# Attention with decay and a softplus FFN on one core: k of each head loaded by two half transfers, and new scheduler tables

## Chip, core, metric

One core of a Trainium2 chip (trn2). The metric is the device time of one execution in microseconds (us); lower is better. The engines are TensorE (PE, with its weight loads shown as PEld), VectorE (DVE), ScalarE (ACT), GpSimd (POOL) and SyncE (SP), which issues nearly all DMAs here. Each engine runs its instructions in order and waits on semaphores.

## What is computed

```python
# q, k, v: (8, 8, 576, 64) float32; f: (8, 8, 576); w_in: (512, 2048), w_out: (2048, 512), float64
scores = q @ k.T / sqrt(64)
cum = cumsum(log(clip(f, 1e-4, 1)))
scores = where(causal, scores + cum[i] - cum[j], -1e9)
attn = exp(scores - max); attn = attn / (sum(attn) + 1e-9)
x = (attn @ v), heads side by side: (4608, 512)
h = x @ w_in
out = softplus(h) @ w_out
```

The batch has 8 sequences of 8 heads, 576 tokens of 64 dimensions each. The host passes q and k transposed, as one array `qkT[b, d, head, q or k, token]`, so that a head's k is 64 rows of 576 floats (2304 bytes).

## The kernel before

**Precision.** Most products are done in a reduced float kind (fp32r), and a float is split into a high part (a rounding copy, "hi") and the rest ("lo", a subtraction). For q and k, both lie twice in a tile of 128 partitions, once in rows 0 to 63 and once in 64 to 127, so that a tile `T` of four planes can be filled with high and low parts in different rows.

**Stages.** The first sequence is done in plain float32 pieces while weights are loaded and split (0 to about 85 us). Then come 56 whole heads (sequences 1 to 7), each a job of `attention`; between their matmuls stand those of the FFN for blocks of 512 tokens that are already finished (85 to 975 us). The last 2048 tokens go through two "super blocks", whose matrix products are arranged as seven products in place of eight (975 us to the end).

**A whole head.** `load` issues the DMAs of q (two transfers of 64 partitions, line 886, in small reversed pieces) and of k (line 891), each into a buffer of the tag `raw`, of which there are two. `prepare` makes `T` from them: casts `T<-k` and `T<-q` through the helper of line 329, on ACT or DVE (128 rows of k, 128 rows of q, and 64 rows of k a second time), and two subtractions on POOL (line 931). When these are done the `raw` buffers are free, and the next head's q and k can be issued. Two rows with the cumulated decay come from `aug_d` into T by DMA (lines 920 and 923). Of `T` there are two buffers.

Then, for each tile of query rows: scores on PE (lines 976, 977, `s<-T`), the mask and the row's minimum of the negated score on DVE (line 981, `s<-s,cmask`, and 1018, `negm`), the weights on ACT (line 1025, `p` for the two short tiles and `pb` for the long ones), sums and scaling (lines 1038, 1039, 1053, 1055, on any of three engines), the transpose on PE (line 1118, `b<-ident,pb`), its high part (`ph`, ACT, or DVE line 1137 for a small block) and low part (`pl`, DVE, line 1140), and the product with v on PE (line 1265, `o`). v is loaded as `vr` (lines 826 and 831) and split into `vhl` (line 903). The FFN's first product is line 1506 (`h`), its gate on ACT is `e` (line 325), split into `gh` and `gl` (line 1550), partly stored to DRAM (`g_d`, line 1554), and the second product is line 1580 (`acc`).

**What sets the order.** Operations are given to a `Plan`, each with the engines that may run it, an estimated cost on each, and what it needs. `run` places one operation after another: of those that are ready in a window of 700, the one whose planned start, less a number for its kind, is smallest. This number is looked up in the table `SOONER`; the table `RATHER` adds to the cost of a kind on one engine and so moves work between engines. The kind is the name of the function that emits it. Planned costs decide only the order; on the chip, semaphores decide when each runs. SP's DMAs are in the planned order as well. The planner counts a DMA of 288 KB as landed 2.1 us after its slot on SP.

```python
    key = s and (s[0] - op.sooner, op.rank)
    return each * (n - 1) + 2.1 + kb / n / RATE - on_dma(kb, n, eng).cost
```

Of the kernel before, what the change touches and what calls it, by code (L numbers as in the profile page):

```python
# [48 lines left out]
S_FROM, S_EACH = 9, 4  # L49

SOONER = {
    "<lambda>": 0.26,
    "attention.finish.shift": 0.15,
    "attention.finish_stats.scale": -0.17,
    "attention.load.k": 0.22,
    "attention.load_quad.<lambda>": 6,
    "attention.load_v.v": 0.21,
    "attention.output_tiled.put": 0.09,
    "attention.prepare.decay_rows": -0.14,
    "attention.split_v.v_hi": -0.68,  # L60
    "attention.split_v.v_lo": -0.04,
    "attention.stat_tile.row_min": 0.04,
    "attention.stat_tile.shift": 0.11,
    "attention.weights.keep": 0.19,
    "attention.weights.spread": -1.63,
    "decay.load": 5.45,
    "decay.split": 2.5,
    "ffn_block.gate.hi_part": -0.27,
    "ffn_block.gate.keep": 3.7,
    "ffn_block.gate.lo_part": -0.52,  # L70
    "ffn_block.gate.raw": -0.12,
    "ffn_block.second.load": 3.23,
    "ffn_block.split_stored.load": 0.22,
    "ffn_block.split_x.lo_part": 0.45,
    "ffn_block.up_part.load": 0.31,
    "load_f64.clip": -0.06,
    "load_f64.join": 0.17,
    "load_f64.low": -0.42,
    "load_f64.scale": 0.22,
    "load_f64.sign": -0.04,  # L80
    "split_w_in.hi_part": 0.13,
    "split_w_in.keep": -0.23,
    "split_w_in.lo_part": -0.23,
    "split_w_out.lo_part": -0.29,
    "store_x.store": 4.21,
    "super_blocks.down_out.keep": -1.38,
    "super_blocks.down_set.split.high": -0.17,
    "super_blocks.gate.raw": 0.07,
    "super_blocks.gate.store": 0.47,
    "super_blocks.lay_out.hold.begin": 0.29,  # L90
    "super_blocks.lay_w.load": 1.48,
    "super_blocks.lay_w.split.lo": 0.55,
    "super_blocks.lay_w.step.go": 0.02,
    "super_blocks.lay_x.less.go": 0.57,
    "super_blocks.lay_x.load": 5.93,
    "super_blocks.lay_x.split.high": 0.36,
    "super_blocks.lay_x.split.low": 0.74,
    "super_blocks.super_block.ups.sum_of.go": 0.07,
    "turn_mask.turn": 6,
}  # L100
RATHER = {
    ("attention.finish_stats.scale", "ACT"): 0.85,
    ("attention.finish_stats.scale", "DVE"): 0.08,
    ("attention.finish_stats.scale", "POOL"): -0.39,
    ("attention.prepare.<lambda>", "ACT"): 0.15,
    ("attention.split_v.v_hi", "ACT"): 0.94,
    ("attention.weights.hi_part", "DVE"): 1.02,
    ("attention.weights.keep", "ACT"): -0.4,
    ("attention.weights.keep", "DVE"): -0.48,
    ("ffn_block.gate.hi_part", "ACT"): 1.61,  # L110
    ("ffn_block.gate.hi_part", "DVE"): 1.87,
    ("load_f64.sign", "POOL"): 1.23,
    ("put_out.<lambda>", "ACT"): 0.87,
    ("set_rows.<lambda>", "DVE"): 1.51,
    ("split_w_in.hi_part", "DVE"): 0.6,
    ("split_w_out.hi_part", "ACT"): 0.42,
    ("split_w_out.hi_part", "DVE"): 0.53,
    ("super_blocks.down_set.split.high", "ACT"): 1.12,
    ("super_blocks.lay_sums.<lambda>", "DVE"): -0.49,
    ("super_blocks.lay_sums.<lambda>", "POOL"): -0.17,  # L120
    ("super_blocks.lay_w.split.hi", "ACT"): -0.75,
    ("super_blocks.lay_w.split.hi", "DVE"): -0.75,
    ("super_blocks.lay_w.split.lo", "POOL"): 1.66,
    ("turn_mask.turn", "DVE"): -0.42,
}


def kind_of(emit):

    return emit.__qualname__.split("<locals>.", 1)[-1].replace("<locals>.", "")  # L130
# [15 lines left out]
class Plan:  # L146
# [14 lines left out]
    def add(self, on, emit, after=(), takes=(), lag=None, loose=False):  # L161
        op = Op(on, emit, after, takes, lag)
        op.loose = loose
        kind = kind_of(emit)
        op.sooner = SOONER.get(kind, 0.0)
        if len(op.on) > 1:
            op.on = [x._replace(bias=x.bias + RATHER.get((kind, x.eng), 0.0)) for x in op.on]
        op.at = len(self.ops)
        op.rank = op.at + self.late
        self.ops.append(op)  # L170
        for t in set(takes):
            self.queue[t].append(op)
        for d in op.after:
            d.users.append(op)
        return op
# [107 lines left out]
def on_dma(kb, n=1, eng="SP"):  # L283

    return On(eng, max(0.6 * n, kb / RATE) if eng == "SP" else 1.5 * n)


def dma_lag(kb, n=1, eng="SP"):
    each = 0.6 if eng == "SP" else 1.5
    return each * (n - 1) + 2.1 + kb / n / RATE - on_dma(kb, n, eng).cost  # L290
# [26 lines left out]
def last_first(x, n=64):  # L317

    *lead, (_, w) = x.ap
    return bass.AP(x.tensor, x.offset + w - n, [*lead, [-n, w // n], [1, n]])  # L320
# [12 lines left out]
def tile_decay_attention_softplus_ffn(  # L333
# [39 lines left out]
                x32=2, ps=2, wl=2, vhl=3, vraw=1, raw=2, one=2)  # L373
    plan = Plan(BUFS | dict(T0=4, stat=4, p=2, xh0=1, xh1=1, xl0=1))
    add, give = plan.add, plan.give

    def joined():
        parts = []

        def row(e):  # L380
            for part in parts:
                part(e)

        op = add(On("PE", 0.0), row)
        op.parts = parts
        return op
# [11 lines left out]
    def add_dma(emit, kb, n=1, eng="SP", **more):  # L398
        return add(on_dma(kb, n, eng), emit, lag=dma_lag(kb, n, eng), **more)
# [9 lines left out]
    def buf(tag, shape, name, dtype=F32):  # L409
        return pool.tile(shape, dtype, tag=tag, name=name, bufs=BUFS[tag])  # L410
# [91 lines left out]
    def exchange(e):  # L502
# [12 lines left out]
            lambda e, x=x, v=v: e.mul(x, ident[0:BH, 0:BH], v) if e is nc.scalar  # L515
# [261 lines left out]
    def attention(job):  # L777

        b, heads = job["b"], job["heads"]
# [29 lines left out]
        st = {}  # L809
# [71 lines left out]
        def load():  # L881
            def q(e):
                st["q"] = buf("raw", [P, S], f"q{n}")
                for r in (0, 64):
                    out = st["q"][r : r + 64].rearrange("p (n t) -> p n t", t=64)
                    e.dma_start(out=out, in_=last_first(qkT[b, :, heads[0], 0]))

            def k(e):
                st["k"] = buf("raw", [P, S], f"k{n}")
                x = qkT[b, :, heads[0], 1]  # L890
                e.dma_start(out=st["k"], in_=bass.AP(x.tensor, x.offset, [[0, 2], *x.ap]))

            st["ql"] = add_dma(q, 288, 2, takes=("raw",))
            st["kl"] = add_dma(k, 288, takes=("raw",))

        def split_v():
            def v_hi(e):
# [427 lines left out]
        def loads():  # L1325
            if quad:
                load_quad()
            elif pair:
                st["T"] = T_of[heads[0]]
                st["vr"], st["V"], st["vtag"] = V_of[heads[0]]  # L1330
            else:
                (load32 if plain else load)()
                load_v()
# [1432 lines left out]
```

## Time and profile before

| | us |
|---|---|
| three runs | 1317.85, 1315.25, 1317.53 (median 1317.53) |
| profiled execution | 1319.71 |
| its span, first to last instruction | 1317.8 |
| mean granted clock of PE | 0.949 |
| PE busy in the span | 1170.3 (89%) |

In a profile's rows, L891 is line 891 of the kernel. In lists of groups, `out<-in` names the tiles, x is the count, and three numbers a/b/c are the shortest, median and longest duration in ns. "Idle before" is time in which the engine stood, and what ended it. In lists of waits the three numbers are us in total, times, and the longest. The chain is the work that ended last, followed back from the end, each step to what released it.

### The profile page before, as it was taken

To read this page: it belongs to the slowest core of one execution; us is meant where nothing else is said; L and a number is where in the kernel's file an instruction comes from. 1 tells how busy PE (TensorE), PEld (TensorE's weight loads), DVE (VectorE), ACT (ScalarE), POOL (GpSimd) and SP (SyncE) were. 2 spreads that over 40 slices of the span, in tenths; PEclk is the share of its full clock that TensorE was granted. 3 is DMA by queue.
4 is the path that set the end of the run, shared out by engine and by line. 5 is a ranking of instruction groups with operands and counts; after the bars stand their busy time and mean duration, and the time that the engine had idled before them with its cause. 6 is when DMAs were issued, how large, how long until landed. Compare 5 with 4: busy or idle time off the path is not lost.

```text
span 1317.8 us, 21604 instructions
## 1 busy us (share of the span) xinstructions
PE 1170.3 (89%) x6764; PEld 989.3 (75%) x6764; DVE 915.1 (69%) x2534; ACT 785.7 (60%) x1906; POOL 449.3 (34%) x445
## 2 busy tenths in 40 slices
PE   9998878898887789887888878888899999999998
PEld 7766677776666677776677667776787878799998
DVE  7877677775565667574565665665767599899784
ACT  7866566666555577665566655665665475554432
POOL 4224455444333335443334332433412014411110
PEclk9999888898889899899898998988999999999999
DMA  8786454344446444444444463544357677644441
GB/s 222 239 228 187 139 161 147 95 146 125 117 117 177 122 142 148 143 127 138 130 139 124 122 178 105 148 138 124 119 188 205 201 234 232 182 136 136 125 136 66
DMA packets 219186, 200.53 MB, mean 152 GB/s; under 512 B 84704, under 2 KB 187392, under 8 KB 219072
## 3 DMA queue, kind: packets, MB, share of 16 engines
q1 hardware_dynamic: 219048, 199.15, 51.2%
q8 instruction: 53, 0.87, 0.3%
q14 instruction: 61, 0.50, 0.1%
q10 hardware_dynamic: 24, 0.02, 0.0%
HBM read 141.17 MB, written 57.84 MB: 151 GB/s over the span
## 4 chain that ended last, share of the span: by engine, by line
PE 38%; DMA 34%; DVE 14%; ACT 5%; POOL 3%; issue 3%; SPq 3%; DVEq 0%; POOLq 0%; ACTq 0%
DMA k<-in_qkT 25%; PE late_E L2387 6%; PE late_E L2050 5%; PE h L1506 4%; PE acc L1580 4%; PE o L1265 3%; DMA vr<-in_vR 3%; PE b L1118 2%; DVE pl L1140 2%; ACT T L329 2%; POOL T L931 2%; PE late_D L2050 1%; PE late_D L2387 1%; PE late_C L2387 1%; PE late_B L2387 1%
## 5 line engine op out<-in xcount | busy, mean ns | idle before, releaser
L981 DVE CUSTOM_DVE_ANT_0 s<-s,cmask 128x288 f32<-128x288 f32 (+6 forms) x320 | 136.8, 443 | 73.1 <-PE s L977 43.9
L931 POOL TENSOR_TENSOR T<-k,T 64x576 fp32r<-64x576 f32 x56 | 80.0, 1429 | 297.4 <-DVE negm L1018 137.0
L1025 ACT ACTIVATE pb<-s,negm 128x288 f32<-128x288 f32 (+5 forms) x272 | 143.4, 530 | 46.0 <-DVE negm L1018 42.0
L976 PE MATMUL s<-T 128*128 128x192 f32 (+1 forms) x336 | 108.2, 328 | 25.7 <-ACT p L1025 8.4
L1140 DVE TENSOR_TENSOR pl<-b,ph 128x512 fp32r<-128x512 f32 x168 | 108.2, 662 | 25.9 <-ACT ph L329 24.8
L329 ACT CAST ph<-b 64x128 fp32r<-64x128 f32 x224 | 103.0, 489 | 38.5 <-PE b L1118 37.3
L1118 PE MATMUL b<-ident,pb 128*128 128x128 f32 (+2 forms) x280 | 50.6, 259 | 68.0 <-DVE ph L1137 52.9
L977 PE MATMUL s<-T 68*128 68x192 f32 (+1 forms) x336 | 103.8, 312 | 4.0 <-DMA T<-aug_d 4.0
L1265 PE MATMUL o<-ph,vhl 128*128 128x512 f32 x336 | 95.4, 321 | 10.2 <-ACT ph L329 4.8
L1025 ACT ACTIVATE p<-s,negm 128x192 f32<-128x192 f32 (+1 forms) x112 | 40.7, 363 | 104.9 <-DVE negm L1018 104.0
L903 POOL TENSOR_TENSOR vhl<-vr,vhl 128x384 fp32r<-128x384 f32 x56 | 58.3, 1041 | 122.2 <-ACT vhl L329 69.8
L1506 PE MATMUL h<-xh,wl 128*128 128x512 f32 (+1 forms) x320 | 99.7, 400 | 0.0
L976 PEld LDWEIGHTS s<-T 128*128 128x128 f32 (+1 forms) x336 | 65.3, 194 | 44.6 <-ACT p L1025 14.6
L1118 PEld LDWEIGHTS b<-ident,pb 128*128 128x128 f32 (+2 forms) x280 | 34.2, 141 | 83.6 <-DVE ph L1137 61.2
L931 POOL TENSOR_TENSOR T<-q,T 64x576 fp32r<-64x576 f32 x56 | 80.7, 1441 | 34.7 <-DVE negm L1018 10.7
L1265 PE MATMUL o<-pl,vhl 128*128 128x512 f32 x224 | 75.6, 381 | 14.0 <-DVE pl L1140 13.6
L1265 PEld LDWEIGHTS o<-ph,vhl 128*128 128x128 f32 x336 | 71.1, 212 | 20.1 <-ACT ph L329 5.1
L1506 PE MATMUL h<-xl,wih 128*128 128x512 f32 (+1 forms) x320 | 86.2, 394 | 0.0
L1118 PE MATMUL b<-halves,pb 128*128 128x128 f32 x512 | 86.0, 286 | 0.0
L1506 PE MATMUL h<-xh,wih 128*128 128x512 f32 (+1 forms) x320 | 85.6, 391 | 0.0
L329 DVE CAST T<-k 128x576 fp32r<-128x576 f32 (+1 forms) x35 | 16.1, 464 | 98.8 <-DMA k<-in_qkT 97.7
L329 ACT CAST T<-k 64x576 fp32r<-64x576 f32 (+1 forms) x77 | 51.4, 673 | 55.4 <-DMA k<-in_qkT 52.0
(749 smaller groups left out, 3583.5 us busy)
## 6 DMA issues: line engine op xcount, KB each, us to landing
wl<-wil_d SPq DMA_DIRECT2D x40, 512.0 KB
raw_d<-e SPq DMA_DIRECT2D x64, 256.0 KB
q<-in_qkT SPq DMA_DIRECT2D x112, 144.0 KB
k<-in_qkT SPq DMA_DIRECT2D x56, 288.0 KB
vr<-in_vR SPq DMA_DIRECT2D x64, 160.0 KB
x_d<-x SPq DMA_DIRECT2D x28, 288.0 KB
g_d<-gh SPq DMA_DIRECT2D x56, 128.0 KB
g_d<-gl SPq DMA_DIRECT2D x56, 128.0 KB
```

The costliest lines, as they stand in the source:

```text
L329: (e.tensor_copy if hasattr(e, "tensor_copy") else e.copy)(out, in_)
L931: e.tensor_sub(t[rows, i, :], st[x][rows], tb[rows, j, :])
L976: e.matmul(o, qA[:, S - end : S - q0], kA[:, a:z], start=True, stop=False)
L977: e.matmul(o, qB[0:ST, S - end : S - q0], kB[0:ST, a:z], start=False, stop=True)
L981: e.tensor_tensor_reduce(out=box["o"], in0=box["o"], in1=cmask[0:n_q, right - w : right], scale=-0.125, scalar=m0 if i else 3.0e38, op0=AL ...
L1025: e.activation(o, box["o"], AF.Softplus, bias=m1, scale=-1.0, accum_out=acc)
L1118: e.transpose(box["ps"][0 : x.shape[1], at : at + one.shape[1]], x, one)
L1140: e.tensor_sub(box["l"], box["ps"][:, 0:w], box["h"].bitcast(F32))
L1265: e.matmul(boxes[gi]["ps"][0:m, a:z], st["vhl"][:, c, 0:m], pbox[which][:, o : o + z - a], start=gi in fresh and which == "h", stop=gi == ...
L1506: e.matmul(o, l, r, start=m == 0, stop=m == 11)
L2050: e.matmul(banks[to], stationary(x, j), at(b, y, j), start=start and m == 0, stop=m == 5, skip_group_check=not start,)
L2387: e.matmul(like(o, y), x, y, start=q == 0 and f_ == 0 and m == 0, stop=q == NQ - 1 and f_ == 1 and m == 2,)
```

## The change

The load of k is written as two transfers. Before, the source was given an outer dimension of 2 with step 0, so that one transfer filled all 128 partitions. Now each half of the partitions has a transfer of its own from the same 64 rows, and the planner counts two issues.

```diff
             def k(e):
                 st["k"] = buf("raw", [P, S], f"k{n}")
-                x = qkT[b, :, heads[0], 1]
-                e.dma_start(out=st["k"], in_=bass.AP(x.tensor, x.offset, [[0, 2], *x.ap]))
+                for r in (0, 64):
+                    e.dma_start(out=st["k"][r : r + 64], in_=qkT[b, :, heads[0], 1])
 
             st["ql"] = add_dma(q, 288, 2, takes=("raw",))
-            st["kl"] = add_dma(k, 288, takes=("raw",))
+            st["kl"] = add_dma(k, 288, 2, takes=("raw",))
```

Both tables have other numbers, nearly all of them; two lines of each:

```diff
-    "attention.load.k": 0.22,
+    "attention.load.k": 1.91,
...
-    "attention.split_v.v_hi": -0.68,
+    "attention.split_v.v_hi": -0.65,
...
+    ("ffn_block.gate.lo_part", "DVE"): 1.72,
...
+    ("split_w_in.hi_part", "ACT"): -1.85,
```

The name of a kind gets a suffix that the plan doesn't set, so kinds stay as they were:

```diff
-        kind = kind_of(emit)
+        kind = kind_of(emit) + getattr(self, "phase", "")
```

Three places of the new order follow (SP, the casts on DVE and ACT, and POOL), all at the same head, whose q and k are numbered 51 (it is issued at 661.55 us and 662.91 us in the profile before). The number behind the last underscore is a running number and differs between the kernels.

On SP, where this head's q and k are issued. Before:

```order
L886 DMA q51_7075<-in_qkT 64x9x64 x2
L891 DMA k51_7095<-in_qkT 128x1x576
L1371 DMA out_0<-ob4_2_7078 128x512
L1554 DMA g_d_98<-gh5_2_7098 128x256
L1554 DMA g_d_98<-gl5_2_7110 128x256
```

Now:

```order
L886 DMA q51_7069<-in_qkT 64x9x64 x2
L891 DMA k51_7072<-in_qkT 64x576 x2
L1348 DMA x_d_99<-x32_5_6899 128x576
L1554 DMA g_d_98<-gh5_2_7093 128x256
L1554 DMA g_d_98<-gl5_2_7095 128x256
```

k stays right behind q; it is two issues, and the store of an earlier sequence's x comes after it, which stood ahead of q before.

The casts, first on DVE, between the row minimum of head 49's first tile (`negm`) and the low parts of head 48's weights (`pl`). Before:

```order
L981 ISA s49_0_0_7125,negm1_76<-s49_0_0_7125,cmask_74 64x64
L981 ISA negm1_76 64x1
L329 CAST T1_1386<-k51_7095 128x576
L1018 TENSOR_SCALAR negm1_76<-negm1_76 64x1
L1137 TENSOR_TENSOR ph48_0_7145<-b48_0_7128,ph48_0_7145 64x128
L1140 TENSOR_TENSOR pl48_1_7163<-b48_1_7131,ph48_1_7154 128x512
```

Now:

```order
L1137 TENSOR_TENSOR ph48_0_7149<-b48_0_7134,ph48_0_7149 64x128
L981 ISA s49_0_0_7131,negm1_76<-s49_0_0_7131,cmask_74 64x64
L981 ISA negm1_76 64x1
L1140 TENSOR_TENSOR pl48_1_7167<-b48_1_7137,ph48_1_7155 128x512
L1140 TENSOR_TENSOR pl48_2_7169<-b48_2_7144,ph48_2_7164 128x448
L1018 TENSOR_SCALAR negm1_76<-negm1_76 64x1
```

The cast of k is no longer on DVE. In the whole program DVE had 35 casts `T<-k` and 12 `T<-q`; now ACT has all 112 and 56 (77 and 44 before). DVE's 47 subtractions `gl` are now on POOL, which had 25 and has 72, while POOL's scalings of line 1055 go from 113 to 55 (`p` from 80 to 28).

And on ACT, around the casts of the same head. Before:

```order
L329 CAST ph48_2_7161<-b48_2_7139 128x448
L1025 ACTIVATE p1_92,lsum1_80<-s49_0_0_7125,negm1_76 64x64
L329 CAST T1_1386<-q51_7075 128x576
L329 CAST T1_1386<-k51_7095 64x576
L329 CAST ph48_3_7186<-b48_3_7169 128x512
```

Now:

```order
L329 CAST ph48_3_7184<-b48_3_7171 128x512
L1025 ACTIVATE p1_92,lsum1_80<-s49_0_0_7131,negm1_76 64x64
L329 CAST T1_1412<-k51_7072 128x576
L329 CAST T1_1412<-q51_7069 128x576
L329 CAST T1_1412<-k51_7072 64x576
L1025 ACTIVATE pb1_94,part1_84<-s49_4_0_7181,negm1_76 128x288
```

Three casts stand in a row where two stood, ahead of the weights of a long tile (`pb`), and the first of them waits for k.

On POOL, ahead of the subtraction of k into T. Before and now:

```order
L903 TENSOR_TENSOR vhl50_7050<-vr50_6916,vhl50_7050 128x6x64
L931 TENSOR_TENSOR T1_1386<-k51_7095,T1_1386 64x576
L931 TENSOR_TENSOR T1_1386<-q51_7075,T1_1386 64x576
L1055 TENSOR_SCALAR p1_92<-p1_92,rsum1_88 64x64
L1550 TENSOR_TENSOR gl5_4_7241<-e5_4_7123,gh5_4_7212 128x512
```

```order
L1550 TENSOR_TENSOR gl5_2_7095<-e5_2_6993,gh5_2_7093 128x512
L903 TENSOR_TENSOR vhl50_7128<-vr50_6978,vhl50_7128 128x6x64
L1550 TENSOR_TENSOR gl5_3_7153<-e5_3_7123,gh5_3_7151 128x512
L931 TENSOR_TENSOR T1_1412<-k51_7072,T1_1412 64x576
L931 TENSOR_TENSOR T1_1412<-q51_7069,T1_1412 64x576
```

Two `gl` of the FFN, each of which needs a gate `e`, now stand ahead of it.

More of the change, by code (lines that the diff above doesn't have):

```diff
@@ L51 @@
 SOONER = {
-    "<lambda>": 0.26,
-    "attention.finish.shift": 0.15,
-    "attention.finish_stats.scale": -0.17,
-    "attention.load.k": 0.22,
[L56 to L59, printed above, removed]
-    "attention.split_v.v_hi": -0.68,
-    "attention.split_v.v_lo": -0.04,
-    "attention.stat_tile.row_min": 0.04,
-    "attention.stat_tile.shift": 0.11,
-    "attention.weights.keep": 0.19,
@@ L65 @@
[L65 to L99, printed above, removed]
+    "attention.finish.shift": 0.19,
+    "attention.finish_stats.scale": -0.22,
+    "attention.load.k": 1.91,
+    "attention.load.q": 0.09,
+    "attention.load_quad.<lambda>": 0.08,
+    "attention.split_v.v_hi": -0.65,
+    "attention.stat_tile.row_min": -0.09,
@@ new lines @@
+    "attention.stat_tile.shift": 0.11,
+    "attention.weights.hi_part": 0.06,
+    "attention.weights.keep": 0.02,
+    "attention.weights.lo_part": 0.14,
+    "attention.weights.spread": -1.39,
+    "decay.load": 0.56,
+    "decay.split": 6,
+    "decay.store": -0.28,
+    "exchange": -0.2,
+    "ffn_block.gate.hi_part": -0.23,
+    "ffn_block.gate.lo_part": 3.3,
+    "ffn_block.second.load": 6,
+    "ffn_block.split_stored.hi_part": -0.16,
+    "ffn_block.split_stored.lo_part": 0.73,
+    "ffn_block.split_x.hi_part": -0.31,
@@ new lines @@
+    "ffn_block.split_x.lo_part": 4.7,
+    "load_f64.join": 0.02,
+    "load_f64.low": -0.83,
+    "load_f64.scale": -0.06,
+    "load_f64.sign": 2.43,
+    "mark": 3.39,
+    "put_out.<lambda>": -0.13,
+    "set_rows.begin": -4,
+    "split_w_in.hi_part": -0.41,
+    "split_w_in.keep": -0.31,
+    "split_w_in.lo_part": -0.2,
+    "split_w_out.hi_part": -0.26,
+    "split_w_out.lo_part": -0.06,
+    "store_x.store": 0.35,
+    "super_blocks.down_out.keep": -0.62,
+    "super_blocks.down_set.<lambda>": 0.64,
@@ new lines @@
+    "super_blocks.down_set.split.high": -0.8,
+    "super_blocks.down_set.split.low": 0.02,
+    "super_blocks.gate.store": 0.18,
+    "super_blocks.lay_sums.high": -0.22,
+    "super_blocks.lay_sums.low": 0.07,
+    "super_blocks.lay_w.split.lo": 0.74,
+    "super_blocks.lay_w.step.go": 0.44,
+    "super_blocks.lay_x.less.go": 0.34,
+    "super_blocks.lay_x.load": 4.63,
+    "super_blocks.lay_x.split.low": 6,
+    "super_blocks.super_block.product.mm": -0.61,
+    "super_blocks.super_block.ups.sum_of.go": 1.97,
@@ L100 @@
 }
 RATHER = {
[L102 to L122, printed above, removed]
@@ L123 @@
-    ("super_blocks.lay_w.split.lo", "POOL"): 1.66,
-    ("turn_mask.turn", "DVE"): -0.42,
+    ("attention.finish_stats.scale", "DVE"): -0.22,
+    ("attention.finish_stats.scale", "POOL"): -0.62,
+    ("attention.prepare.<lambda>", "ACT"): -1.44,
+    ("attention.weights.hi_part", "DVE"): 1.8,
+    ("attention.weights.keep", "ACT"): -1.73,
+    ("ffn_block.gate.hi_part", "DVE"): -0.72,
+    ("ffn_block.gate.lo_part", "DVE"): 1.72,
+    ("ffn_block.split_stored.hi_part", "ACT"): 0.82,
+    ("ffn_block.split_x.hi_part", "ACT"): -0.15,
@@ new lines @@
+    ("ffn_block.split_x.hi_part", "DVE"): 0.76,
+    ("load_f64.sign", "ACT"): -0.47,
+    ("put_out.<lambda>", "ACT"): -2,
+    ("split_w_in.hi_part", "ACT"): -1.85,
+    ("super_blocks.lay_sums.<lambda>", "DVE"): -0.17,
+    ("super_blocks.lay_w.split.hi", "DVE"): -0.21,
+    ("super_blocks.lay_w.split.lo", "DVE"): 0.07,
+    ("super_blocks.lay_w.split.lo", "POOL"): 0.25,
+    ("super_blocks.lay_w.step.go", "DVE"): -0.52,
+    ("super_blocks.lay_w.step.go", "POOL"): 0.74,
+    ("super_blocks.lay_x.split.high", "ACT"): -1.69,
@@ L125 @@
+    ("super_blocks.lay_x.split.high", "DVE"): -1.79,
 }
```

## The prediction

> **What bounds the kernel now.** I read the page first, then one window for each stage, the waits, and one head row by row.
>
> ```profile
> PE 1170.3 (89%) x6764; PEld 989.3 (75%) x6764; DVE 915.1 (69%) x2534; ACT 785.7 (60%) x1906; POOL 449.3 (34%) x445
> ...
> PE   9998878898887789887888878888899999999998
> ...
> PEclk9999888898889899899898998988999999999999
> ...
> PE 38%; DMA 34%; DVE 14%; ACT 5%; POOL 3%; issue 3%; SPq 3%; DVEq 0%; POOLq 0%; ACTq 0%
> DMA k<-in_qkT 25%; PE late_E L2387 6%; PE late_E L2050 5%; PE h L1506 4%; PE acc L1580 4%; PE o L1265 3%; DMA vr<-in_vR 3%; PE b L1118 2%; DVE pl L1140 2%; ACT T L329 2%; POOL T L931 2%; PE late_D L2050 1%; PE late_D L2387 1%; PE late_C L2387 1%; PE late_B L2387 1%
> ```
>
> TensorE is busy 89% overall, full at both ends, with holes in the middle where the granted clock dips too. A quarter of the chain that ended last is the load of k. By stage (columns: busy time of each engine, granted clock, share of the 16 DMA engines, GB/s):
>
> ```profile
> 0.00:85.00 85.00, 81.97 (x569) 63.74 (x570) 69.00 (x230) 64.58 (x152) 28.57 (x58) 1.00 0.81 235
> 85.00:975.00 890.00, 753.55 (x4092) 623.93 (x4090) 574.73 (x1757) 554.39 (x1437) 354.54 (x321) 0.93 0.47 138
> 975.00:1318.00 343.00, 334.74 (x2108) 301.62 (x2106) 271.37 (x549) 166.75 (x317) 66.17 (x67) 1.00 0.56 167
> ```
>
> The stage with the 56 whole heads, 85 to 975, has PE idle for 890 - 753.55 = 136 us, and a clock of 0.93 costs another 0.07 x 890 = 62 us. Who waits:
>
> ```profile
> DVE T L329 <- DMA k<-in_qkT: 97.7, 27, 5.9
> ...
> PE b L1118 <- DVE ph L1137: 52.9, 20, 4.8
> ACT T L329 <- DMA k<-in_qkT: 52.0, 16, 6.2
> ...
> PE o L1265 <- DVE pl L1140: 18.0, 13, 4.9
> ```
>
> DVE and ACT stand 149.7 us in front of 43 of the k loads; PE then waits for what DVE would have made (ph, pl). One such head, timeline first, then two windows of it:
>
> ```profile
> 662.91 0.53 SPq L891 DMA_DIRECT2D k<-in_qkT  x1
> ...
> 672.21 0.46 DVE L329 CAST T<-k 128x576 fp32r<-128x576 f32 x1 [5.70 <-DMA k<-in_qkT]
> ...
> 673.09 0.46 PE L1118 MATMUL b<-ident,pb 68*128 68x68 f32 x2 [4.54 <-DVE ph L1137]
> ```
>
> ```profile
> 667.00:673.00 6.00, 1.55 (x8) 0.95 (x6) 0.76 (x3) 1.08 (x4) 0.10 (x1) 1.00 0.13 52
> 673.20:676.50 3.30, 3.30 (x13) 2.97 (x14) 3.23 (x7) 2.61 (x6) 3.07 (x3) 0.50 0.19 47
> ```
>
> k takes 672.21 - 662.91 = 9.3 us from issue to its first reader. While everything waits, 0.13 x 16 = 2.1 DMA engines work, at 52 GB/s: the load runs on two of them. Its 128 x 2304 B = 295 KB take 5.7 us at that rate. Behind the gap PE has half its clock for 3.3 us, so a hole is paid twice.
>
> **The change part by part.** *The load of k.* Two transfers with 64 partitions outermost replace one whose source starts with a count of 2. The trace has no such k load. The nearest row for a transfer whose outermost dimension isn't 2 is late_T<-raw_d, 256 KB, at the end:
>
> ```profile
> 1242.56 0.36 SPq L2300 DMA_DIRECT2D late_T<-raw_d  x1
> ...
> 1245.18 0.43 DVE L2320 TENSOR_TENSOR fX<-late_T 128x256 f32<-128x256 f32 x1 [1.27 <-DMA late_T<-raw_d]
> ...
> L891 SPq DMA_DIRECT2D k<-in_qkT x56: 526/541/817, 85.4 to 936.9; - x56
> ```
>
> It was read 2.62 us after its issue. With one issue of 0.36 us ahead, the new k lands after about 3.0 us in an idle queue. As the upper end I only replace the 5.7 us by the rate of the first stage (235 GB/s at 0.81 busy, 290 in full, 1.0 us): 9.3 - 4.7 = 4.6 us. I take 3.5, nearer to the row. Either way 4.7 to 6.3 us go, more than the mean wait (149.7 / 43 = 3.5 us) and about its longest (5.9 and 6.2). The two engines also carry a share of all that SP issues behind k, which now lands sooner; I add nothing for that. SP pays 56 x (2 x 0.36 - 0.54) = 10 us more, in time in which it waits for buffers anyway; if that cover were gone, 0.2 us a head.
>
> *What is the stage worth without the wait?* Not 149.7 us: PE takes over. Three stretches where k came nearly in time give PE's pace, and a longer one where it still cost a little gives the other end:
>
> ```profile
> 444.00:540.00 96.00, 85.18 (x481) 70.34 (x479) 66.18 (x210) 66.78 (x175) 40.43 (x37) 1.00 0.49 150
> 345.00:380.00 35.00, 33.16 (x185) 27.44 (x183) 22.44 (x73) 23.41 (x62) 7.83 (x6) 0.99 0.46 128
> 470.00:500.00 30.00, 28.08 (x162) 23.63 (x161) 21.97 (x76) 23.38 (x62) 12.73 (x12) 1.00 0.52 160
> 570.00:610.00 40.00, 38.79 (x225) 32.25 (x223) 29.93 (x98) 28.11 (x75) 18.52 (x17) 1.00 0.52 158
> ```
>
> ```profile
> DVE T L329 <- DMA k<-in_qkT: 10.2, 4, 4.1
> ```
>
> (The last row is of 444 to 540 alone.) The three: 105 us for 572 matmuls, 0.1836 us each; times the stage's 4092 gives 751 us, a gain of 139. The longer one: 96 / 481 = 0.1996, times 4092 gives 817 us, a gain of 73, and DVE still waits 10.2 us for k in it. The middle is 106; I take 100, a little under, because the three were picked for having no holes and so hold none of the waits that come next.
>
> On the clock, those stretches stand at 0.99 to 1.00. [...]
>
> *The tables.* In the whole program ACT takes all 168 casts of q and k into T, and POOL all 72 of gl:
>
> ```profile
> L329 ACT CAST T<-k x77: 659/672/699, 120.7 to 948.5; 64x576 fp32r<-64x576 f32 x48, 128x576 fp32r<-128x576 f32 x29
> ...
> L329 DVE CAST T<-k x35: 443/459/726, 97.1 to 946.2; 128x576 fp32r<-128x576 f32 x27, 64x576 fp32r<-64x576 f32 x8
> L329 DVE CAST T<-q x12: 442/460/1609, 122.4 to 806.9; 128x576 fp32r<-128x576 f32 x12
> ...
> L1550 DVE TENSOR_TENSOR gl<-e,gh x47: 671/691/1223, 204.1 to 941.0; 128x512 fp32r<-128x512 f32 x47
> ...
> L1550 POOL TENSOR_TENSOR gl<-e,gh x25: 1254/1297/1745, 171.3 to 956.9; 128x512 fp32r<-128x512 f32 x25
> ...
> L1055 POOL TENSOR_SCALAR p<-p,rsum x80: 433/689/1815, 139.4 to 973.2; 64x64 f32<-64x64 f32 x48, 128x192 f32<-128x192 f32 x32
> ```
>
> ACT gains 47 x 0.67 = 31 us and DVE loses 47 x 0.46 = 22; POOL gains 47 x 1.30 = 61 and DVE loses 47 x 0.69 = 32; POOL gives up 58 of its scalings of p and pb, at least 52 x 0.69 = 36. In a stage of 790 us ACT would be at (554 + 31) / 790 = 74% and POOL at (355 + 61 - 36) / 790 = 48%: neither is a bound by its sum, and I cost the moves at nothing beyond the 6 us kept back. Their cover is PE's queue of FFN matmuls between two heads; without it each head pays up to the 2.0 us of its three casts in a row. A gain would be that DVE no longer stands before k at all, its ph and pl staying free; that is inside the 139. The first and last stages are 97% busy on PE; reordering there I put at 0, between -8 (all of the last stage's idle time) and +5.
>
> Sum: the profiled execution took 1319.7 us (span 1317.8 and 1.9 around it), 2.2 over the median of the runs. 1319.7 - 100 = 1219.7, or 1218 on the median's scale.
>
> **The rivals.** *The next wait takes over* (chance 0.22). POOL's queue is in order, and in the new order two gl and a vhl stand ahead of T's subtraction of k (L931); gl waits for a gate that waits for PE. If that costs PE 0.7 to 1.5 us in each of 56 heads, 39 to 84 us of the 106 come back: 1319.7 - 67 to 1319.7 - 22, so 1250 to 1298. For it: DVE has 35% and ACT 38% of this stage free, less once it is shorter, and the L931 chain is what frees the buffers of q and k. Against: POOL is at 40% now.
>
> *The halves land no sooner* (0.04). If what limited k were not its spread over engines but its 128 rows as such, two halves would move the same rows through the same engines, and nothing changes but the tables: 1317 give or take 5. Against stands the 0.13 while nothing else ran. [...]
>
> *Slower* (0.05): ACT becomes what PE waits for. ACT is in order and makes the softmax weights p and pb. With T's three casts in a row (3 x 0.67 = 2.0 us) directly behind a p and ahead of the pb, and on ACT for every head, a k that is still late holds every weight behind it. If each of the 56 heads lost the 2.0 us on PE and half of the 3.3 us at half clock, 3.65 us, the cost is 204 against 106 to 139 gained: 1319.7 + 65 to + 98, about 1385 to 1418. It decides from a loss of 1.9 us a head (106 / 56); less ends in the first rival. It needs k to land later than the 4.6 us above.
>
> **How the numbers follow.** My forecast, k off the path and PE the bound, has 0.65 and its own range is 1319.7 - 139 to - 73, 1180 to 1247. Below that lies 0.04: the -8 of the last stage, or stretches better than those picked. The range 1180 to 1285 leaves out this, the 0.05 and 0.04 of the last two rivals and some 0.04 of the first rival's upper end: 0.17. A change of under 0.2% can't be told from none here. Faster is 0.65 + 0.04 + 0.22 = 0.91; the halves that land no sooner are about as often within 0.2% as not, so same is 0.03 and slower 0.06.
>
> **What would show it.** Right: k leaves the head of the chain's list; ACT's waits for k fall from 149.7 us on both engines to under 20; k's issue to its first cast takes 3 to 5 us where the cast waits; stage 85 to 975 shortens to about 790 us with the clock at 0.98 or more and PE some 90% busy (753.55 less the 62 us, or 4092 x 0.175, over 790). Wrong: k still lands after 9 us (second rival); k lands early but POOL's or ACT's waits in front of T grow and PE stays at 85% (first); PE's waits name ACT p or pb behind T's casts (third). The prediction also fails if the picked stretches owe their pace to work that had been made ready during a hole before them.

## Result and the profile after

The changed kernel takes 1124.9 us (median of 4 runs, 1123.4 to 1128.7) against 1316.4 before: ratio 0.855, 95% interval 0.853 to 0.858. That is 191 us less, where 100 were forecast and 1180 was the low end of the range. The page of the profile after, those lines that stand for the ones shown of before:

```profile
PE 1101.8 (98%) x6764; PEld 950.3 (85%) x6764; DVE 883.7 (79%) x2445; ACT 811.0 (72%) x2014; POOL 471.6 (42%) x426
...
PE   9999999999999999999999999999999999999998
...
PEclk9999999999999999999999999999999999999999
...
PE 81%; DVE 11%; DMA 3%; ACT 3%; issue 1%; SPq 0%; POOL 0%; DVEq 0%; ACTq 0%; POOLq 0%
PE acc L1580 17%; PE h L1506 14%; PE b L1118 7%; PE late_E L2387 7%; PE late_E L2050 6%; PE o L1265 6%; PE s L976 3%; PE s L977 3%; PE h L1485 2%; PE s L971 2%; PE late_B L2387 2%; PE late_D L2050 2%; PE late_D L2387 2%; PE late_C L2387 2%; PE late_A L2387 2%; PE late_C L2050 1%
```

The holes in PE's row are gone, so is the dip of the clock, and DMA went from 34% of the chain to 3%. The windows of the two later stages (same columns as before):

```profile
85.00:780.00 695.00, 685.55 (x4086) 583.47 (x4085) 552.47 (x1688) 570.01 (x1520) 383.60 (x309) 1.00 0.60 177
780.00:1121.00 341.00, 333.42 (x2105) 301.61 (x2103) 263.90 (x541) 170.51 (x328) 59.22 (x60) 1.00 0.56 168
```

4086 matmuls, the stage of whole heads but for six, now take 695 us in place of 890, with 9.5 us of idle PE in place of 136. The last stage went from 343 to 341: all of the gain is in the stage with the heads.

How k lands, on the chain, and the wait of ACT for it in the list of waits:

```profile
132.01 3.01 DMA k<-in_qkT
```

```profile
ACT T L329 <- DMA k<-in_qkT: 0.9, 3, 0.5
```

The second half lands 3.01 us after its own issue; the first was issued 0.62 us ahead of it (131.39). So in this head k takes 3.6 us from the first issue, where 3.5 was put down. In the first head, where ACT waits as well, k is read 5.4 us after its first issue. The 149.7 us that DVE and ACT stood before k are 0.9.

### The profile page after: what moved, and what is told of

Same layout as the page of the kernel before. It is cut to its first block, busy times and chain, and to the rows that moved or that the text cites. A ratio compares the mean times of both kernels' runs of the same rounds, so it can differ in the third digit from the quotient of the medians.

```text
span 1121.6 us, 21642 instructions
## 1 busy us (share of the span) xinstructions
PE 1101.8 (98%) x6764; PEld 950.3 (85%) x6764; DVE 883.7 (79%) x2445; ACT 811.0 (72%) x2014; POOL 471.6 (42%) x426
## 4 chain that ended last, share of the span: by engine, by line
PE 81%; DVE 11%; DMA 3%; ACT 3%; issue 1%; SPq 0%; POOL 0%; DVEq 0%; ACTq 0%; POOLq 0%
PE acc L1580 17%; PE h L1506 14%; PE b L1118 7%; PE late_E L2387 7%; PE late_E L2050 6%; PE o L1265 6%; PE s L976 3%; PE s L977 3%; PE h L1485 2%; PE s L971 2%; PE late_B L2387 2%; PE late_D L2050 2%; PE late_D L2387 2%; PE late_C L2387 2%; PE late_A L2387 2%; PE late_C L2050 1%
## 5 line engine op out<-in xcount | busy, mean ns | idle before, releaser
L981 DVE CUSTOM_DVE_ANT_0 s<-s,cmask 128x448 f32<-128x448 f32 (+6 forms) x320 | 138.2, 435 | 53.5 <-PE b L1118 26.7
L1550 POOL TENSOR_TENSOR gl<-e,gh 128x512 fp32r<-128x512 f32 x72 | 94.7, 1316 | 102.2 <-DVE gh L329 42.9
L976 PE MATMUL s<-T 128*128 128x192 f32 (+1 forms) x336 | 99.7, 304 | 4.3 <-ACT p L1025 2.4
L1506 PE MATMUL h<-xh,wl 128*128 128x512 f32 (+1 forms) x320 | 89.5, 374 | 0.0
L1265 PE MATMUL o<-ph,vhl 128*128 128x512 f32 x336 | 87.9, 299 | 0.4 <-DVE pl L1140 0.2
L329 ACT CAST T<-k 128x576 fp32r<-128x576 f32 x112 | 75.2, 673 | 3.8 <-PE s L976 1.7
L1580 PE MATMUL acc<-woh_dt_float32r,gh 128*128 128x512 f32 x176 | 71.9, 409 | 0.0
L1055 DVE TENSOR_SCALAR pb<-pb,rsum 128x576 f32<-128x576 f32 (+2 forms) x86 | 69.8, 823 | 1.1
L1265 PEld LDWEIGHTS o<-ph,vhl 128*128 128x128 f32 x336 | 63.5, 189 | 7.8 <-DVE pl L1140 1.0
L1580 PE MATMUL acc<-woh_dt_float32r,gl 128*128 128x512 f32 x176 | 69.3, 394 | 0.0
```

The costliest lines, as they stand in the source:

```text
L329: (e.tensor_copy if hasattr(e, "tensor_copy") else e.copy)(out, in_)
L976: e.matmul(o, qA[:, S - end : S - q0], kA[:, a:z], start=True, stop=False)
L981: e.tensor_tensor_reduce(out=box["o"], in0=box["o"], in1=cmask[0:n_q, right - w : right], scale=-0.125, scalar=m0 if i else 3.0e38, op0=AL ...
L1265: e.matmul(boxes[gi]["ps"][0:m, a:z], st["vhl"][:, c, 0:m], pbox[which][:, o : o + z - a], start=gi in fresh and which == "h", stop=gi == ...
L1506: e.matmul(o, l, r, start=m == 0, stop=m == 11)
L1580: e.matmul(st["acc", tt], l, r[fc], start=first and m == 0, stop=last and m == 2,)
```

## The experiments

The two parts of the change were first taken apart: the old or the new instruction order was kept exactly, and the transfer alone exchanged in it.

**Old tables, new k.** The kernel before, order and planner cost untouched, with the new transfer alone:

```diff
-                x = qkT[b, :, heads[0], 1]
-                e.dma_start(out=st["k"], in_=bass.AP(x.tensor, x.offset, [[0, 2], *x.ap]))
+                for r in (0, 64):
+                    e.dma_start(out=st["k"][r : r + 64], in_=qkT[b, :, heads[0], 1])
```

> The kernel before with k loaded by two half transfers and every table, cost and instruction order as before: only the transfer differs. Theory 'transfer' (k's late landing on two DMA engines, and what queues behind it there, made nearly all of the 191 us): 1125 to 1150 us, PE's idle time in the stage of whole heads under 40 us of the 136 before. Theory 'tables' (the order by the old tables has waits of its own once k is early, as the prediction's picked stretches held 5% of idle time): 1180 to 1245 us, around the 1218 forecast, and the rest of the way to 1125 is the tables' work.

Measured: 1148.6 us, ratio to before 0.877 (0.873 to 0.880). The transfer by itself gives 163 us, with 23 us of idle PE left in the stage:

```profile
85.00:800.00 715.00, 692.06 (x4063) 582.56 (x4062) 573.89 (x1748) 546.39 (x1429) 355.13 (x318) 0.99 0.59 171
```

'Transfer' holds and 'tables' falls: in an order that was made while k was late, PE still runs at 97%.

**New tables, old k.** The changed kernel with the old transfer put back, same order as the changed kernel.

> The changed kernel with k loaded by the one transfer with a repeating source, same order as the changed kernel: only the tables are new. Theory 'transfer': 1290 to 1345 us, k read 9 us after its issue again, now with ACT standing before it in most of the 56 heads (some 150 us in sum). Theory 'tables': well under before, 1180 to 1260 us, as DVE no longer stands before k and PE is fed by it.

Measured: 1292.9 us, 0.988 (0.984 to 0.992) of before. The tables alone give 19 us, and with the new transfer 24 (1148.6 to 1124.9). With the old k it is ACT that stands before it:

```profile
ACT T L329 <- DMA k<-in_qkT: 139.0, 47, 7.4
```

**Is it the two engines, or the repeating source?** In the changed kernel each half was cut once more, without any repeat:

```diff
                 for r in (0, 64):
-                    e.dma_start(out=st["k"][r : r + 64], in_=qkT[b, :, heads[0], 1])
+                    for i_, z_ in ((0, 62), (62, 64)):
+                        e.dma_start(out=st["k"][r + i_ : r + z_], in_=qkT[b, i_:z_, heads[0], 1])
```

> The changed kernel with each half of k cut into 62 and 2 partitions: four transfers, none with a repeating source, same order otherwise. 62 has no divisor from 3 to 16, so by the reading that the outermost count decides on how many DMA engines a transfer runs, nearly all of k is on two engines again. Theory 'engines': k is read 8 to 10 us after its issue and the time is that of the changed kernel with the old transfer (e2), within 25 us. Rival 'repeat' (a source that repeats is slow in itself, whatever the engines): 1125 to 1140 us, with the control (48 and 16) the same.

> Control for the cut into 62 and 2: each half cut into 48 and 16 partitions, which 16 engines share evenly; again four transfers. Both theories: 1125 to 1140 us, some us over the changed kernel for two more issues of about 0.5 us on SP in each of 56 heads. If it is slow as well, the number of transfers and not the engines made the cut into 62 and 2 slow.

> The changed kernel with each half of k cut into 57 and 7 partitions; 57 = 3 x 19, so by the reading 'engines' 114 of the 128 rows run on three DMA engines, 38 rows each at 0.09 us, 3.4 us in place of 5.7. k is then read some 2.3 us sooner than with 62 and 2. Theory 'engines': between the two, 1150 to 1230 us, ACT's waits for k 30 to 70 us in sum in place of 108. Rival: 1300 us, as any odd cut is slow; or 1125 to 1135, as 2.3 us are enough to hide k.

Measured: 62 and 2, 1308.3 us; 57 and 7, 1188.4; 48 and 16, 1128.9. ACT's waits for k, of the first and then of the second kernel:

```profile
ACT T L329 <- DMA k<-in_qkT: 107.9, 38, 5.8
```

```profile
ACT T L329 <- DMA k<-in_qkT: 42.0, 25, 4.1
```

The control with as many transfers costs 4 us; the cut into 62 costs 183 with no repeat in its source. So a repeat isn't needed for the loss, and the number of transfers isn't what is slow. Where a cast waits for k, it is read 9.0 to 11.1 us after its first issue with 62 rows (8.9 to 11.7 in the kernel before), and 6.0 to 9.1 us after it with 57. The reading 'engines' of the three expectations, two DMA engines for 62 rows, three for 57 and 16 for 48, agrees with the three times in order; for 62 and 48 the number of engines was not measured. For 57 rows the trace has it, while ACT waits for k until 385.51 us:

```profile
382.70:384.70 2.00, 2.00 (x11) 1.63 (x10) 0.86 (x5) 0.59 (x2) 1.43 (x1) 1.00 0.20 74
```

0.20 x 16 = 3.2 engines move 74 GB/s, where in the hole before 2.1 engines moved 52. In the changed kernel, while most rows of the k issued at 131.39 move (133 to 134 us), the share is 0.98, or 15.7 engines, with 280 GB/s. So what goes with the loss in these runs is the number of DMA engines that k's rows run on.

**Late k, or blocked engines?** The prediction counted the wait for k and nothing for what stands behind it on the same two engines. To tell these apart, the new k was kept and a spare transfer of the old form was issued behind it, into a DRAM tile that nobody reads (it is work added, and no result depends on it):

```diff
+                x = qkT[b, :, heads[0], 1]
+                e.dma_start(out=spare_d[bh], in_=bass.AP(x.tensor, x.offset, [[0, 2], *x.ap]))
```

> The changed kernel with one more transfer behind each head's k: the same repeating source, 295 KB on two DMA engines, into a DRAM tile that nobody reads. k itself lands as in the changed kernel; the two engines are blocked for some 5.7 us behind it, as they were before. Theory 'blocked engines' (what SP issues behind k, as v, the weights wl, the stored gates g_d and the rows of aug_d, came late through the two engines and that made part of the 191 us): 1150 to 1230 us. Theory 'k alone' (only the wait for k itself cost): 1125 to 1140 us.

Measured: 1271.2 us, 146 over the changed kernel, above the range that either theory gave. The waits of this kernel:

```profile
DVE vhl L329 <- DMA vr<-in_vR: 51.3, 16, 7.1
...
ACT vhl L329 <- DMA vr<-in_vR: 26.8, 11, 6.6
...
PE s L980 <- DMA T<-aug_d: 16.0, 5, 4.6
ACT T L329 <- DMA k<-in_qkT: 13.8, 11, 3.5
```

k is nearly in time (13.8 us in place of 139.0), and now v (`vr`) and the decay rows come late, with longest waits of 7.1 and 4.6 us. PE's stage looks as with the old k, with 106 us of idle time and the lower mean clock:

```profile
85.00:935.00 850.00, 744.49 (x4128) 618.77 (x4127) 553.74 (x1697) 576.23 (x1528) 380.00 (x309) 0.93 0.55 166
```

So of the 168 us between old and new k under the new tables (1292.9 to 1124.9), the spare transfer brings 146 back with k nearly in time; with the old k in place of it the time is 22 us higher. The same in the old order:

> The kernel before, order and all, with the new k and the full spare transfer behind it (295 KB on two DMA engines into a DRAM tile that nobody reads): k lands early, the two engines stay blocked as long as before. It splits the 163 us that the transfer gave in the old order (1311.8 to 1148.6). Theory 'blocked engines': most of them come back, 1250 to 1295 us, with waits for v, wl and aug_d in place of those for k. Theory 'k alone', as the prediction counted: 1150 to 1170 us.

Measured: 1273.3 us, 0.967 (0.960 to 0.975) of before: 125 of the 163 us return. Its largest waits for transfers in the stage:

```profile
ACT vhl L329 <- DMA vr<-in_vR: 47.5, 19, 6.0
ACT woh_dt_float32r L329 <- DMA wi_d<-woh_dt_float: 32.2, 6, 8.0
```

'Blocked engines' holds in both orders: they are enough for most of the loss. What a late k would cost with free engines was not tried, so it is open how much of the loss a late k alone would bring, and the 146 and 125 us are not a share that is left when k's part is taken off.

Part of the blocking lies on SP itself. In the trace before, a store of g_d takes 3.99 us to issue, where the median of its line is 0.41, and meanwhile 0.12 x 16 = 1.9 DMA engines work:

```profile
307.54 3.99 SPq L1554 DMA_DIRECT2D g_d<-gh  x1
```

```profile
309.00:311.50 2.50, 2.50 (x20) 2.21 (x19) 1.46 (x5) 1.14 (x5) 0.00 (x0) 1.00 0.12 48
```

SP's next transfer, the g_d of gl, is issued at 311.63, 0.10 us after the end of that issue; what SP has still to issue stands behind it. Over the whole trace, issues of more than 1 us are 59 with 130 us in sum before and 17 with 23 after; with the new tables and the old k they are 77 with 179, and in the changed kernel with the full spare 92 with 241. What held each of them is not in the trace, but by this count the spare blocks more than the old k did, so its 146 us may be too high for the old k's own blocking. It also writes to DRAM and not to the core's memory. A spare of the same size over 16 engines, to price the added work by itself, was not run; nor is it known how much comes from held issues and how much from data that lands late.

Half the spare:

> The changed kernel with a spare transfer of half the size behind each k (32 rows twice, 147 KB on two DMA engines into a DRAM tile that nobody reads): the two engines are blocked for some 2.9 us a head in place of 5.7. Theory 'blocked engines' with slack (a transfer may come late by some us before anyone waits; 57 rows on three engines, 3.4 us, cost 63 us in place of 183): 1140 to 1190 us. Rival, in proportion to the time blocked: half of the full spare's 146 us, 1198.

Measured: 1164.9 us, 40 over the changed kernel, where proportion would give 73. So a blocking of some 3 us a head mostly finds slack, and one of some 6 us doesn't (both are estimates, from 147 and 295 KB at the 52 GB/s of the hole before).

**Which table?** Both kernels have the new k with its planner cost of two issues; the last one is their control, with both tables old.

> The kernel before with the new k and its planner cost, the new table SOONER and the old RATHER: the order within the engines is searched anew, the choice of engines is not. If the 24 us between the old order with the new k (1148.6) and the changed kernel (1124.9) come from the order: 1125 to 1135. If from the moves between engines (casts of T to ACT, gl to POOL): 1143 to 1155.

> The kernel before with the new k and its planner cost, the new table RATHER and the old SOONER. If the 24 us come from the moves between engines: 1125 to 1135; if from the order: 1143 to 1155. If the two tables only work together, both kernels are over 1140, or worse than the old pair.

> The old tables with the new k and the planner's cost for two issues, as in the two kernels with one new table each (the first kernel with the old tables kept the old cost, and so the old order). Control for those two. If one new table beside an old one is worse than the old pair: near 1149, up to 1156, under both. If the order by the new cost with the old tables is what was bad: 1165 to 1180, and then the new SOONER changed nothing and the new RATHER gained 10.

Measured: new `SOONER` alone 1177.1 us, new `RATHER` alone 1162.6, both old 1158.1. The new `SOONER` beside the old `RATHER` is 19 us worse than the old pair; the new `RATHER` beside the old `SOONER` differs from it by 5 us, which is within the noise (ratios to before 0.885 and 0.883, each give or take 0.004). Neither is better alone; together they are 33 better (1124.9). The control itself lies between the two ranges that were written for it, up to 1156 and from 1165. The planner's cost alone, one number, took the old pair from 1148.6 to 1158.1 (ratios 0.877 and 0.883, whose intervals just overlap). The gain of the tables is that of a fitted pair and has no single place.

**A second repeating source.** Line 831 loads 64 short rows of v twice in the same form; it was split as well in the changed kernel:

```diff
-                        x = vR[b, heads[0], 0:64, 0]
-                        twice = bass.AP(x.tensor, x.offset, [[0, 2], *x.ap])
-                        e.dma_start(out=vr[:, NCH], in_=twice)
+                        for r in (0, 64):
+                            e.dma_start(out=vr[r : r + 64, NCH], in_=vR[b, heads[0], 0:64, 0])
```

> The changed kernel with the other repeating source, the 64 short rows of v at line 831 (32 KB, 128 pieces of 256 bytes on two engines, some 1.3 us a head), as two half transfers too, same order. Theory 'blocked engines': those two engines are free 1.2 us earlier, but PE has only 9.4 us of idle time left in the stage: 1120 to 1125 us, a gain of 0 to 5. Rival: SP's extra issue (56 x 0.3 us or more) comes late to wl and g_d and costs 0 to 5 us.

Measured: 1122.8 us (6 runs, 1122.1 to 1125.1), ratio to before 0.856 (0.853 to 0.859). Against the changed kernel's 1124.9 (1123.4 to 1128.7), measured beside other runs of before, this is no difference that can be told.

## Why the prediction was wrong

*Direction, bound and the load itself were right.* k was on the path, ran on two engines (0.13 x 16 = 2.1), lands in 3.6 us now (3.5 forecast, 3.0 to 4.6 as bounds; 5.4 in one other wait), and PE took over as the bound. The clock is at 1.00 (0.98 or more), ACT's waits for k are 0.9 us (under 20). But PE is 99% busy in the stage, where some 90% was written, and the stage takes 695 us, not 790.

*The step that failed is what the stage is worth without the wait.* It took three stretches "where k came nearly in time" as PE's own pace, with 5% of idle time. k still made waits in them. The waits of the stretch 345 to 380 in the trace of before:

```profile
DVE T L329 <- DMA k<-in_qkT: 1.9, 1, 1.9
...
PE b L1118 <- DVE ph L1137: 1.1, 1, 1.1
...
PE o L1265 <- DVE pl L1140: 0.7, 2, 0.4
```

470 to 500, with the same releasers:

```profile
DVE T L329 <- DMA k<-in_qkT: 2.1, 1, 2.1
...
PE b L1118 <- DVE ph L1137: 1.0, 1, 1.0
...
PE o L1265 <- DVE pl L1140: 0.8, 1, 0.8
```

In 570 to 610 DVE waits 1.8 us for k as well and PE 0.9 for ph and pl. PE is idle for 1.84, 1.92 and 1.21 us in the three, 4.97 us of 105, and 4.2 of these stand behind a ph or pl that DVE made after it had waited for that head's k. That k caused all 4.2 is not shown: in the old order with the new k, PE is still idle for 3.2% of the stage (22.94 of 715 us), against 4.7% here. With the busy time alone, 100.03 / 572 x 4092 = 716 us, the gain would have been 174.

The 195 us of the stage come out so: 100 forecast; 39 taken off the 139 by hand for "the waits that come next", which didn't come on top (the old order with the new k has 23 us of idle PE, less than the 36 that the stretches give); 36 of idle time taken for PE's own (4.97 / 572 x 4092); and 20 because PE is busy for only 0.1678 us a matmul (685.55 / 4086) against 0.1749 in the picked stretches, 29 us in sum, less the 9.5 us that are still idle. The old order with the new k has 0.1703 (692.06 / 4063), so some 19 of the 29 need no new table. By the durations in the traces, matmuls of one line and shape last as long in the stretches as they do after, but the stretches held a mix that is longer by 1.6% (mean 338 ns, 333 in the stage after); that is some 11 of the 29 us, an estimate. Why the rest is shorter is open.

*A term was set to nothing without a reason.* "The two engines also carry a share of all that SP issues behind k ... I add nothing for that." The spare transfers show that such blocking is enough for 146 and 125 us with k nearly in time. It may bear on the 39 us above: waits that come next for transfers held by the same two engines would go together with k's. No run separates that. The chain and the waits of before named k for nearly everything, probably because whoever stood before k found the other late transfers already there; that was argued and not measured.

*The tables* were put at 0, with 6 us kept back. They gave 24 with the new k and 19 with the old. SP's two issues of k take 0.59 us each (median) and not 0.36, 35 us in place of the 10; no price for it is seen. ACT at 570 / 695 = 82% and POOL at 55% are fuller than reckoned and still no bound; the rival of POOL's queue didn't come, nor did that of ACT's casts in a row. That halves land no sooner was refuted: the transfer alone took the time from 1311.8 to 1148.6 us; the one transfer that they replace ran on 2.1 engines, and most rows of the halves move at a share of 0.98 of the 16.

## What to carry to other kernels

Look at the outermost count of a transfer, and at the DMA share while something waits for it: here the broadcast with 2 in front came at a share of 0.13, 57 rows at 0.20 and the halves of 64 rows at 0.98, and k cut into 62 rows was read as late as the broadcast (9.0 to 11.1 us after its first issue). Such a transfer can cost more than its own lateness: with the spare behind the new k, v was waited for 78 us in all (51.3 on DVE and 26.8 on ACT; 5.1 in the changed kernel), and in the trace before SP stood for 3.99 us in an issue behind k's. The list of waits names only the transfer that came last at each wait. An issue that takes microseconds in SP's timeline (3.99, where 0.41 is the median) is a second sign. When a bound is read from good stretches of a trace, take their idle time apart too: ask in each whether the same wait is still in it, and set the pace by busy time alone as the far end of the range.

## What was not expected of the hardware

A spare transfer of the old form behind each k, by estimate two of 16 DMA engines for 5.7 us a head (295 KB at the 52 GB/s of the old k), costs a kernel at 98% PE 146 us, with k nearly in time (13.8 us of waits); half its size costs 40, and k itself on 3.2 engines, by estimate for 3.4 us (38 rows each at 0.09 us), 63. SP was seen to stand for 3.99 us in an issue whose median is 0.41, while 1.9 engines worked. About a third of the price of the holes is the clock, by estimate: it was 0.93 in the stage with holes before and with the full spare, and 1.00 in that of the changed kernel, so in the trace before 0.07 x 890 = 62 us beside 136 us of idle time.
